# Moving output stores from ScalarE's DMA ring into GpSimd's, with the instruction order planned anew

## The chip, the cores and the metric

One core of one Trainium2 chip. The metric is the device time of one execution in microseconds; a kernel is quoted by the median of its runs. A ratio below is the mean time of one kernel's fast runs over the mean of the other kernel's fast runs of the same rounds, so it is not quite the ratio of the medians. "Slow" runs (here, runs over 1.5% above the fastest of the same kernel) are left out of ratios. Each ratio comes with a 95% interval. By a margin of 2% every experiment below but two counts as "same" as the kernel before (5 is slower, 6 is unclear); smaller differences are claimed only where the interval leaves out 1. The profile's span is some 2 us shorter than the device time of the same run.

## The reference, cut to what matters

```python
# 4 sequences, 8 heads, 768 positions, head size 64
scores = q @ k.T / 8 - slope[h] * dist             # a local window of 96 positions and 8 global ones
a = softmax(where(keep, scores, -1e9))
x = (a @ v).transpose(0, 2, 1, 3).reshape(3072, 512)
h = x @ w_in                                       # 512 -> 2048
out = (h - tanh(h)) @ w_out                        # 2048 -> 512, float32, [3072, 512]
```

The kernel cuts the 3072 rows into 24 tiles of 128. A tile's attention touches only its own and the preceding block of keys (and the 8 global ones), so the two dense layers are most of the matmul work. Two words recur: a "ring" is the queue of the transfers (DMA) that one engine issues, and an "eviction" copies a finished product out of PSUM, the memory in banks that matmuls write to.

## The kernel before

Every engine's instruction order is decided while the kernel is built: `plan()` plays through all operations with assumed durations and always takes next the one that could start first. Only these parts matter here (cuts are marked):

```python
opool = ctx.enter_context(tc.tile_pool(name="opool", bufs=4))     # four output tiles
kpool, bpool = ...                                                # qk: 7, kq: 5 buffers
...
def load_bf(u, nm):                                # q, k, v of tile u: GpSimd's ring, cast to bf16
    ... nc.gpsimd.dma_start(out=dst..., in_=by_head)
def a_DT(u):                                       # transpose of q and k by DMA: SyncE's ring
    nc.sync.dma_start_transpose(out=qk[u]..., in_=kq.pop(u)...)
def m2_e(u, part, eng):                            # eviction: PSUM -> ot, on ScalarE or VectorE
    ots[u] = opool.tile([P, DM], FP32, name="ot")
    copy_on(eng)(out=ots[u][:, lo:hi], in_=os_.pop((u, part)))
def store(u, part):                                # ot -> HBM, 256 KB
    eng = nc.sync if u == NU - 1 else nc.scalar
    eng.dma_start(out=out[...], in_=ots[u][:, lo:hi])
...
bufs = {"mo": 3, "kq": KQ, "p0": 3, "p1": 3, "x": 3, "xT": NG, "g": NG, "th": 3, "ot": 4}
```

With four `ot` buffers, the eviction of tile u has to wait until the store of tile u-4 has landed. The plan knows this rule.

The softmax here doesn't subtract the row's maximum and nothing guards it: scores larger than these inputs give would overflow.

Of the kernel before, what the change touches and what calls it, by code (L numbers as in the profile page):

```python
# [15 lines left out]
def kernel(  # L16
# [11 lines left out]
    nc = tc.nc  # L28

    B, H, S, Dh = q.shape  # L30
# [3 lines left out]
    NU = B * NQ  # L34
# [147 lines left out]
    ops = {}  # L182
    w_in_r = moe_w_in.rearrange("(c p) f -> p c f", p=P)
    w_out_r = moe_w_out.rearrange("(c p) d -> p c d", p=P)
    PE, ACT, DVE, POOL, SP = ENG.PE, ENG.Activation, ENG.DVE, ENG.Pool, ENG.SP
# [6 lines left out]
    def op(key, eng, us, fn, after=(), take=(), give=(), hold=(), free=(), pri=0, dma=0.0, alt=None, at=None, slack=0.0):  # L192
        ops[key] = dict(
            key=key, at=at, slack=slack, eng=eng, us=us, fn=fn, alt=alt, after=[a for a in after if a is not None],
            take=list(take), give=list(give), hold=list(hold), free=list(free), pri=pri, dma=dma,
        )
# [258 lines left out]

    def store(u, part):
        lo, hi = parts(u)[part]
        eng = nc.sync if u == NU - 1 else nc.scalar
        eng.dma_start(out=out[SEQ[u] * P : (SEQ[u] + 1) * P, lo:hi], in_=ots[u][:, lo:hi])


    AHEAD = 5.5
    YIELD = 0.0
    HALVES = 99
    EB = 2
    INF = 1.0e9
    NUDGE = {
        ('AV', 21): -0.3,
        ('E', 12, 1): 0.3,
        ('E', 13, 0): 0.3,  # L470
        ('E', 13, 1): -0.6,
        ('E', 14, 1): -0.6,
        ('E', 17, 0): -0.15,
        ('E', 17, 1): -0.15,
        ('E', 18, 1): 0.15,
        ('E', 21, 1): 1.0,
        ('E', 9, 1): -0.3,
        ('M', 14, 1): 0.3,
        ('M', 20, 0): 1.0,
        ('M', 9, 1): 1.0,  # L480
        ('R', 15): 0.6,
        ('R', 9): -0.3,
        ('S', 3, 0): 0.15,
        ('S', 6, 0): 1.0,
        ('S', 7, 0): 0.6,
        ('V', 16): -0.15,
        ('V', 19): -0.6,
        ('V', 4): -0.3,
        ('X', 6): 0.15,
        ('Xe', 9): -0.3,  # L490
        ('ev', 7, 0): 1.0,
        ('g', 1, 6): 0.3,
        ('g', 11, 6): 0.6,
        ('g', 13, 14): 0.3,
        ('g', 2, 2): 0.6,
        ('g', 7, 14): 1.0,
        ('g', 7, 8): 0.6,
        ('g', 9, 2): 1.0,
        ('m1', 12, 0): 0.6,
        ('m1', 4, 4): -0.3,  # L500
        ('m1', 4, 8): -0.15,
        ('m1', 5, 0): -0.3,
        ('m1', 5, 4): -0.3,
        ('m1', 5, 8): -0.15,
        ('m1', 6, 2): 0.6,
        ('m1', 8, 6): 1.0,
        ('m1', 9, 8): 0.6,
        ('m2', 1, 2): 1.0,
        ('m2', 10, 0): 1.0,
        ('m2', 11, 0): -0.3,  # L510
        ('m2', 12, 3): 0.3,
        ('m2', 15, 1): 0.3,
        ('m2', 2, 1): 1.0,
        ('m2', 21, 1): 0.6,
        ('m2', 3, 0): 0.6,
        ('m2', 3, 2): 1.0,
        ('m2', 5, 3): 1.0,
        ('m2', 7, 1): 0.3,
        ('m2', 7, 3): 0.3,
        ('m2', 8, 0): 1.0,  # L520
        ('st', 12, 0): 0.6,
        ('st', 8, 0): 1.0,
        ('th', 6, 10): -0.6,
        ('th', 7, 10): 0.3,
        ('th', 9, 8): 0.15,
    }
    SLACK_DT, SLACK_DX = 4.0, 4.0
    WARM = (1.1, 7.0)
    COLD = 6.3
    FETCH = (15.8, 0.9)  # L530
    T_ROWS, T_LD, T_W, T_ST, T_DT, T_DX = 0.67, 0.89, 1.3, 0.7, 1.75, 0.9
    LOADS = "ttttiiitiiiotoooioitooo"
    first, n_of = [], {"t": 0, "i": 0, "o": 0}
    for c in LOADS + "t" * NU:
        if n_of[c] < (NU if c == "t" else WJ):
# [12 lines left out]
    for it in first:  # L548
# [3 lines left out]
        u = it[1]  # L552
        for nm in ("vf", "kf", "qf") if u == 0 else ("kf", "qf", "vf"):
            key = ("ld", nm, u)
# [4 lines left out]
            after = []  # L559
            if nm == "vf" and u >= B + NV:  # L560
# [3 lines left out]
                 after=after, take=["kq"] if nm == "kf" else [], slack=0.15)  # L564
# [36 lines left out]
    for u in range(NU):  # L601
# [8 lines left out]
        if u < PE_T:  # L610
            t_us = 0.47 if PLAIN <= u < ROWS else 0.24
            apart = u < APART
            for j, r in ((1, rk), (0, rq)):
# [5 lines left out]
                     lambda eng, u=u, j=j: a_Te(u, j, eng),  # L619
# [40 lines left out]
        b, at, n_b = block_of(u)  # L660
# [9 lines left out]
    for g, us in enumerate(groups):  # L670
        b, o, n, _ = shape1(g)
# [10 lines left out]
    for u in range(NU):  # L682
        g = group_of[u]
        last_f = {f: f0 for f0, m in chunks(g) for f in range(f0, f0 + m)}
        n_u = 4 * len(parts(u))
        for n in range(n_u):
            part, qq = divmod(n, 4)
            lo, hi = parts(u)[part]
            op(("m2", u, n), PE, 4 * ((hi - lo) / 2400.0 + 0.0025), lambda u=u, n=n: m2(u, n),
               after=[("out", (4 * qq + 3) // FJ)] + [("g", g, f) for f in sorted({last_f[f] for f in range(4 * qq, 4 * qq + 4)})],  # L690
               take=["mo"] if u < EARLY2 and qq == 0 else [], hold=[(("m2", u, part), 1)] if qq == 0 else [],
               give=["g"] if n == n_u - 1 and ends_block(u) else [], pri=2)
        for part in range(len(parts(u))):
            alt = [(DVE, 0.3)] if part else [(ACT, 0.5), (DVE, 0.56)]
            flex(("ev", u, part), alt, lambda eng, u=u, part=part: m2_e(u, part, eng),
                 after=[("m2", u, 4 * part + 3)], take=["ot"] if part == 0 else [],
                 give=["mo"] if u < EARLY2 else [], free=[("m2", u, part)], pri=1)
            op(("st", u, part), SP if u == NU - 1 else ACT, 0.1 if u == NU - 1 else 0.4, lambda u=u, part=part: store(u, part), after=[("ev", u, part)],
               give=["ot"] if part == len(parts(u)) - 1 else [], dma=T_ST)


    def plan():
# [18 lines left out]
                b[i : i + n] = [INF] * n  # L721
            return at, got

        ring = {SP: [0.0, []], POOL: [5.8, []]}
        share = {SP: 0.5, POOL: 0.5}
        done, start, width = {}, {}, {}
        f1 = f2 = 0.0
        queues = {}
        for u in range(NU):
# [14 lines left out]
        while ready or any(queues.values()):  # L744
# [11 lines left out]
                    cand.append((qu[0], 10 ** 6 + name[1]))  # L756
            due = INF
            for key in ready:
                if key not in since:
                    since[key] = max([0.0] + [start[a[1]] if a[0] == "issue" else done[a] for a in ops[key]["after"]])  # L760
                if key[0] == "S" and len(ops[key]["hold"]) > 2:
                    due = min(due, since[key] + YIELD)
            for key, n in cand:
                o = ops[key]
                eng = o["eng"]
                if o["alt"]:
                    eng = min(o["alt"], key=lambda x: free[x[0]] + 0.6 * x[1])[0]
                t = free[eng]
                via = POOL if o["eng"] is POOL else SP
                if o["dma"] and len(ring[via][1]) >= 8:  # L770
                    t = max(t, sorted(ring[via][1])[-8])
                if key not in since:
                    since[key] = max([0.0] + [start[a[1]] if a[0] == "issue" else done[a] for a in o["after"]])
                t = max(t, since[key])
                if key[0] == "m1" and t >= due:
                    continue
                if best is not None and round(t + NUDGE.get(key, 0.0), 3) > best[0][0]:
                    continue
                if o["hold"]:
                    w = find(o["hold"])[0]  # L780
                    if w is None:
                        continue
                    t = max(t, w)
                for p in set(o["take"]):
                    n_p = o["take"].count(p)
                    if len(avail[p]) < n_p:
                        t = None
                        break
                    t = max(t, sorted(avail[p])[n_p - 1])
                if t is None:  # L790
                    continue
                c = (round(t + NUDGE.get(key, 0.0), 3), o["pri"], n)
                if best is None or c < best[0]:
                    best = (c, key, t, eng)
# [10 lines left out]
            if o["at"]:  # L805
                done[key] = o["at"]
            elif o["dma"]:
                via = POOL if o["eng"] is POOL else SP
                mine, other, part = ring[via], ring[SP if via is POOL else POOL], share[via]
                begin = max(mine[0], end + (1.0 if via is SP else 1.97))  # L810
                both = min(max(0.0, other[0] - begin), o["dma"] / part)
                mine[0] = begin + o["dma"] + both * (1 - part)
                if begin < FETCH[0] <= mine[0]:
                    mine[0] += FETCH[1]
                other[0] += both * part
                done[key] = mine[0] + (0.8 if via is SP else 0.45) + o["slack"]
                mine[1].append(done[key])
            else:
                done[key] = end + LAT[o["eng"]]
            if o["hold"]:  # L820
# [11 lines left out]
                    continue  # L832
                bank[banks[label] : banks[label] + width[label]] = [done[key]] * width[label]
            for p in o["take"]:
                avail[p].remove(min(avail[p]))
            for p in o["give"]:
                avail[p].append(done[key])
            order.append((t, key))
            if key[0] == "m1":
                queues["m1", min(key[1], EARLY)].pop(0)  # L840
# [74 lines left out]
```

## Time and profile before

215.21 us (median of 4 runs, 214.77 to 215.94).

| view | before | how to read it |
|---|---|---|
| span | 212.3 us | first to last instruction |
| TensorE busy | 203.8 us | near the limit; the gaps are what a change of order can win |
| TensorE waiting for DMA transposes | 1.9 us in 2 waits | the only stalls in mid-kernel |
| share of the 16 DMA engines in 46 to 73 us | 1.92 packets in flight on average | full; loads, transposes and stores compete |
| landing of a store, median and longest | 3.4 and 8.6 us | no eviction waits for one. The median is over all 26 store transfers; the 12 issued before 132 us, while the rings are full, took 6.1 to 8.6 us |

Lines of this profile stand in the prediction.

### The profile page before, as it was taken

The page shows a single profiled execution, that of the slowest core. Times are in us where ns is not written, and L with a number is a line of the kernel's source. Part 1 is how long each engine was busy: PE and PEld are TensorE (multiplying, and loading weights), DVE is VectorE, ACT ScalarE, POOL GpSimd, SP SyncE. Part 2 cuts the span into 40 slices and gives each one's busy share as a digit, 9 for nine tenths or more (in the row PEclk, how much of TensorE's full clock was granted, in tenths as well). Part 3 has the DMA queues.
Part 4 walks back from the last instruction along what each step waited for, and adds up shares of the span by engine and source line. Part 5 has one row for each costly group of instructions (what it writes and reads, how often), then busy time and mean ns, then how long its engine had stood idle before and what let it go on. Part 6 is the DMA issues. An engine that isn't in the chain of part 4 may idle for free.

```text
span 212.3 us, 5296 instructions
## 1 busy us (share of the span) xinstructions
PE 203.8 (96%) x2172; PEld 145.4 (68%) x2198; DVE 132.1 (62%) x269; ACT 120.4 (57%) x184; POOL 71.9 (34%) x92
## 2 busy tenths in 40 slices
PE   7899999999799899999999999999999999999994
PEld 2679995984466767577677578757755786666754
DVE  6579796656475777385667487757655594343611
ACT  4777865553446786487358465667545773444410
POOL 8995676667344365345342700000000000000000
PEclk9999999999999999999999999999999999999999
DMA  5999999999999999999999999212362220110112
GB/s 181 182 189 177 180 203 180 187 157 167 159 158 186 151 137 181 144 181 184 153 169 164 165 142 193 50 74 53 99 112 90 77 49 0 52 51 16 37 49 100
DMA packets 106073, 27.49 MB, mean 129 GB/s; under 512 B 94656, under 2 KB 103104, under 8 KB 106048
## 3 DMA queue, kind: packets, MB, share of 16 engines
q0 software_dynamic: 74048, 13.11, 84.9%
q1 hardware_dynamic: 28144, 7.48, 26.6%
q10 hardware_dynamic: 3856, 6.56, 9.7%
q8 instruction: 17, 0.28, 0.6%
q14 instruction: 8, 0.07, 0.1%
HBM read 27.26 MB, written 6.29 MB: 158 GB/s over the span
## 4 chain that ended last, share of the span: by engine, by line
PE 82%; DMA 13%; DVE 1%; issue 1%; POOL 0%; ACT 0%; SPq 0%; DVEq 0%
PE ps L410 38%; PE ps L444 32%; DMA qk<-kq 6%; DMA kq<-in_q_dram 5%; PE ps L314 5%; PE ps L342 2%; DMA kf<-in_k_dram 2%; PE ps L346 2%; PE ps L277 1%; PE ps L281 1%; PE ps L369 1%; PE ps L165 1%; POOL kq L242 0%; DVE kh L296 0%; DVE g L429 0%
## 5 line engine op out<-in xcount | busy, mean ns | idle before, releaser
L410 PE MATMUL ps<-xT,w_in_bf 128*128 128x256 bf16 (+1 forms) x960 | 93.0, 251 | 0.1
L444 PE MATMUL ps<-w_out_bf,g 128*128 128x512 bf16 (+3 forms) x391 | 87.3, 362 | 1.6 <-issue 0.5
L410 PEld LDWEIGHTS <-w_in_bf 128*128 128x128 bf16 x960 | 77.5, 98 | 13.3 <-DMA w_in_bf<-in_moe_w_in_dram 0.3
L429 DVE TENSOR_TENSOR g<-ps,th 128x512 bf16<-128x512 f32 (+1 forms) x102 | 64.9, 656 | 28.5 <-ACT th L422 27.8
L422 ACT ACTIVATE th<-ps 128x512 f32<-128x512 f32 (+1 forms) x102 | 56.8, 573 | 38.1 <-PE ps L410 35.0
L444 PEld LDWEIGHTS <-g 128*128 128x128 bf16 x416 | 37.9, 98 | 33.7
L323 ACT ACTIVATE pd<-ps 128x1024 bf16<-128x1024 f32 x24 | 24.4, 1024 | 14.0 <-PE ps L314 14.0
L236 POOL DMA_DIRECT2D vb<-in_v_dram x24 | 21.4, 894 | 14.3 <-DMA kq<-in_k_dram 4.6
L242 POOL DMA_DIRECT2D kq<-in_k_dram x20 | 17.7, 886 | 23.6 <-DMA qk<-kq 16.4
L323 ACT ACTIVATE po<-ps 128x1024 bf16<-128x1024 f32 x20 | 20.2, 1023 | 6.1 <-PE ps L314 6.1
L242 POOL DMA_DIRECT2D kq<-in_q_dram x20 | 17.7, 886 | 7.8 <-DMA vb<-in_v_dram 7.6
L329 DVE TENSOR_TENSOR pd<-pd,mk 128x1024 bf16<-128x1024 bf16 x20 | 13.8, 690 | 6.2 <-ACT pd L323 6.2
L355 DVE TENSOR_TENSOR x<-ps,rden 128x512 bf16<-128x512 f32 x24 | 16.6, 692 | 0.8
L454 ACT COPY ot<-ps 128x512 f32<-128x512 f32 x16 | 9.4, 585 | 13.7 <-PE ps L444 13.7
L329 DVE TENSOR_TENSOR po<-po,mk 128x1024 bf16<-128x1024 bf16 x20 | 13.7, 687 | 2.7 <-ACT po L323 2.7
L342 PE MATMUL ps<-vb,pd 128*128 128x65 bf16 x192 | 14.1, 193 | 0.0
L342 PEld LDWEIGHTS <-pd 128*128 128x128 bf16 x192 | 12.5, 98 | 1.4 <-issue 0.2
L454 DVE COPY ot<-ps 128x512 f32<-128x512 f32 (+3 forms) x10 | 5.8, 585 | 12.0 <-PE ps L444 11.9
L314 PEld LDWEIGHTS <-qk 64*128 64x128 bf16 x288 | 8.1, 94 | 7.0 <-issue 4.0
L314 PE MATMUL ps<-qk 64*128 64x128 bf16 x288 | 10.8, 217 | 1.9 <-DMA qk<-kq 1.9
L346 PE MATMUL ps<-vb,po 128*128 128x65 bf16 x160 | 12.4, 193 | 0.0
L346 PEld LDWEIGHTS <-po 128*128 128x128 bf16 x160 | 10.4, 97 | 1.1
(48 smaller groups left out, 81.9 us busy)
## 6 DMA issues: line engine op xcount, KB each, us to landing
out_dram<-ot ACTq DMA_DIRECT2D x23, 256.0 KB, 6.1
vb<-in_v_dram POOLq DMA_DIRECT2D x24, 128.0 KB, 10.9
kq<-in_k_dram POOLq DMA_DIRECT2D x22, 128.0 KB, 11.2
kq<-in_q_dram POOLq DMA_DIRECT2D x22, 128.0 KB, 11.2
w_in_bf<-in_moe_w_in_dram POOLq DMA_DIRECT2D x8, 256.0 KB, 8.3
w_out_bf<-in_moe_w_out_dram POOLq DMA_DIRECT2D x8, 256.0 KB, 8.7
kf<-in_k_dram SPq DMA_DIRECT2D x2, 256.0 KB, 4.5
qf<-in_q_dram ACTq DMA_DIRECT2D x2, 256.0 KB, 3.7
```

The source lines that it names most:

```text
L236: i = nc.gpsimd.dma_start(out=v_of(u)[:, :, 0:Dh], in_=by_head)
L242: i = nc.gpsimd.dma_start(out=dst.rearrange("p (h d) -> p h d", d=Dh), in_=by_head)
L314: nc.tensor.matmul(s[:, slot(2 * p + hh), :], kT(prev_of[u] if o else u)[r, p, :], qk[u][r, 0, p, :], start=u >= B, stop=True, skip_group_ ...
L323: nc.scalar.activation(pr[u, o].rearrange("q (a h) f -> q a h f", a=2)[:, part], sc[u, o][:, part, :].rearrange("q a (h f) -> q a h f", f= ...
L329: nc.vector.tensor_tensor(out=pr[u, o], in0=pr[u, o], in1=mk[:, :, mask_of(u, o) - 1, :], op=ALU.mult)
L342: nc.tensor.matmul(dst, pr[u, 0][:, slot(h), :], v_of(u)[:, h, :], start=True, stop=last,)
L346: nc.tensor.matmul(dst, pr[u, 1][:, slot(h), :], v_of(prev_of[u])[:, h, :], start=False, stop=True,)
L355: nc.vector.tensor_tensor(out=xs[u].rearrange("q (a h) d -> q a h d", a=2), in0=t[:, :, :, 0:Dh], in1=rden.to_broadcast([P, 2, H // 2, Dh] ...
L410: nc.tensor.matmul(t[:, (f - f0) * n : (f - f0 + 1) * n], w_in_bf[j][:, c, fo : fo + P], xT[b][:, c, o : o + n], start=(c == 0), stop=(c = ...
L422: nc.scalar.activation(h_view(ths[g, f0], g, m), h_view(hs[g, f0], g, m), AF.Tanh, bias=0.0, scale=1.0)
L429: nc.vector.tensor_tensor(out=gs[b][:, f0 : f0 + m, o : o + n], in0=h_view(hs.pop((g, f0)), g, m), in1=h_view(ths.pop((g, f0)), g, m), op= ...
L444: nc.tensor.matmul(os_[u, part][:, 0 : hi - lo], gs[b][:, f, t * P : (t + 1) * P], w_out_bf[f // FJ][:, f % FJ, lo:hi], start=(f == 0), st ...
```

## The change

The intent is to take the stores out of the competition that delays the transposes: 21 of 24 go into GpSimd's ring, behind the loads, and the planner now follows all three rings as fluids that share the DMA engines, re-estimating every landing at each issue. The 58 hand-found nudges make room for two, and the loads of weights are ordered a little differently.

```diff
-        eng = nc.sync if u == NU - 1 else nc.scalar
+        eng = nc.sync if u == NU - 1 else nc.gpsimd if u < BY_POOL else nc.scalar    # BY_POOL = 21
...
     NUDGE = {
-        ('AV', 21): -0.3,
...                                                 # 57 more
+        ('AV', 8): -0.6,
+        ('T1', 0): 1.0,
     }
-    T_ROWS, T_LD, T_W, T_ST, T_DT, T_DX = 0.67, 0.89, 1.3, 0.7, 1.75, 0.9
-    LOADS = "ttttiiitiiiotoooioitooo"
+    T_ROWS, T_LD, T_W, T_ST, T_DT, T_DX = 0.67, 0.89, 1.3, 0.65, 1.05, 0.55
+    SHARE = {  # speed of (GpSimd, SyncE, ScalarE) rings, by which of them are active
...
+    LOADS = "tttitiiitiiootooiiotooo"
...
+        def fly(jobs, t, t_end): ...               # moves all transfers in flight forward
+        def fly_from(q, key, t, end): ...          # a new issue: new landings for all of them
```

More of the change, by code (lines that the diff above doesn't have):

```diff
@@ L457, in store @@
         lo, hi = parts(u)[part]
-        eng = nc.sync if u == NU - 1 else nc.scalar
+        eng = nc.sync if u == NU - 1 else nc.gpsimd if u < BY_POOL else nc.scalar
         eng.dma_start(out=out[SEQ[u] * P : (SEQ[u] + 1) * P, lo:hi], in_=ots[u][:, lo:hi])
     AHEAD = 5.5
+    BY_POOL = 21
     YIELD = 0.0
@@ L467 @@
     NUDGE = {
-        ('AV', 21): -0.3,
-        ('E', 12, 1): 0.3,
-        ('E', 13, 0): 0.3,
-        ('E', 13, 1): -0.6,
-        ('E', 14, 1): -0.6,
-        ('E', 17, 0): -0.15,
-        ('E', 17, 1): -0.15,
-        ('E', 18, 1): 0.15,
-        ('E', 21, 1): 1.0,
-        ('E', 9, 1): -0.3,
-        ('M', 14, 1): 0.3,
-        ('M', 20, 0): 1.0,
-        ('M', 9, 1): 1.0,
-        ('R', 15): 0.6,
-        ('R', 9): -0.3,
-        ('S', 3, 0): 0.15,
-        ('S', 6, 0): 1.0,
-        ('S', 7, 0): 0.6,
-        ('V', 16): -0.15,
-        ('V', 19): -0.6,
-        ('V', 4): -0.3,
-        ('X', 6): 0.15,
-        ('Xe', 9): -0.3,
-        ('ev', 7, 0): 1.0,
-        ('g', 1, 6): 0.3,
-        ('g', 11, 6): 0.6,
-        ('g', 13, 14): 0.3,
-        ('g', 2, 2): 0.6,
-        ('g', 7, 14): 1.0,
-        ('g', 7, 8): 0.6,
-        ('g', 9, 2): 1.0,
-        ('m1', 12, 0): 0.6,
-        ('m1', 4, 4): -0.3,
-        ('m1', 4, 8): -0.15,
-        ('m1', 5, 0): -0.3,
-        ('m1', 5, 4): -0.3,
-        ('m1', 5, 8): -0.15,
-        ('m1', 6, 2): 0.6,
-        ('m1', 8, 6): 1.0,
-        ('m1', 9, 8): 0.6,
-        ('m2', 1, 2): 1.0,
-        ('m2', 10, 0): 1.0,
-        ('m2', 11, 0): -0.3,
-        ('m2', 12, 3): 0.3,
-        ('m2', 15, 1): 0.3,
-        ('m2', 2, 1): 1.0,
-        ('m2', 21, 1): 0.6,
-        ('m2', 3, 0): 0.6,
-        ('m2', 3, 2): 1.0,
-        ('m2', 5, 3): 1.0,
-        ('m2', 7, 1): 0.3,
-        ('m2', 7, 3): 0.3,
-        ('m2', 8, 0): 1.0,
-        ('st', 12, 0): 0.6,
-        ('st', 8, 0): 1.0,
-        ('th', 6, 10): -0.6,
-        ('th', 7, 10): 0.3,
-        ('th', 9, 8): 0.15,
+        ('AV', 8): -0.6,
+        ('T1', 0): 1.0,
     }
-    SLACK_DT, SLACK_DX = 4.0, 4.0
+    SLACK_DT, SLACK_DX = 2.0, 2.0
     WARM = (1.1, 7.0)
@@ L530 @@
     FETCH = (15.8, 0.9)
-    T_ROWS, T_LD, T_W, T_ST, T_DT, T_DX = 0.67, 0.89, 1.3, 0.7, 1.75, 0.9
-    LOADS = "ttttiiitiiiotoooioitooo"
+    T_ROWS, T_LD, T_W, T_ST, T_DT, T_DX = 0.67, 0.89, 1.3, 0.65, 1.05, 0.55
+    RING = 5.8
+    TAIL = {POOL: 0.45, SP: 0.8, ACT: 0.8}
+    SHARE = {
+        (True, False, False): (1.0, 0, 0), (False, True, False): (0, 1.0, 0), (False, False, True): (0, 0, 1.0),
+        (True, True, False): (0.36, 0.42, 0), (True, False, True): (0.5, 0, 0.42), (False, True, True): (0, 0.5, 0.42),
+        (True, True, True): (0.3, 0.29, 0.2),
+    }
+    LOADS = "tttitiiitiiootooiiotooo"
     first, n_of = [], {"t": 0, "i": 0, "o": 0}
@@ L697 @@
                  give=["mo"] if u < EARLY2 else [], free=[("m2", u, part)], pri=1)
-            op(("st", u, part), SP if u == NU - 1 else ACT, 0.1 if u == NU - 1 else 0.4, lambda u=u, part=part: store(u, part), after=[("ev", u, part)],
+            by = SP if u == NU - 1 else POOL if u < BY_POOL else ACT
+            op(("st", u, part), by, {SP: 0.1, POOL: 0.7, ACT: 0.4}[by], lambda u=u, part=part: store(u, part), after=[("ev", u, part)],
                give=["ot"] if part == len(parts(u)) - 1 else [], dma=T_ST)
@@ L722, in find, with fly @@
             return at, got
-        ring = {SP: [0.0, []], POOL: [5.8, []]}
-        share = {SP: 0.5, POOL: 0.5}
         done, start, width = {}, {}, {}
+        flying, landed, at_dma = {POOL: [], SP: [], ACT: []}, {POOL: [], SP: [], ACT: []}, [0.0]
+        def fly(jobs, t, t_end):
+            fin = {}
+            while t < t_end:
+                if FETCH[0] <= t < FETCH[0] + FETCH[1]:
+                    t = min(FETCH[0] + FETCH[1], t_end)
+                    continue
+                heads = [q for q in jobs if jobs[q] and jobs[q][0][1] <= t]
+                later = min([jobs[q][0][1] for q in jobs if jobs[q] and jobs[q][0][1] > t] + [t_end])
+                if not heads:
+                    t = later
+                    continue
+                rate = SHARE[tuple(q in heads for q in (POOL, SP, ACT))]
+                rate = {q: r for q, r in zip((POOL, SP, ACT), rate)}
+                dt = min([later - t] + [jobs[q][0][2] / rate[q] for q in heads])
+                if t < FETCH[0]:
+                    dt = min(dt, FETCH[0] - t)
+                t += dt
+                for q in heads:
+                    jobs[q][0][2] -= dt * rate[q]
+                    if jobs[q][0][2] < 1e-6:
+                        key = jobs[q].pop(0)[0]
+                        fin[key] = t + TAIL[q] + ops[key]["slack"]
+            return fin
@@ new lines, in fly_from @@
+        def fly_from(q, key, t, end):
+            busy = flying[POOL]
+            done.update(fly(flying, at_dma[0], t))
+            at_dma[0] = max(at_dma[0], t)
+            begin = end + (2.0 if q is POOL else 1.0)
+            if key[0] in ("T", "Xe"):
+                begin = t + (4.2 if busy else 2.2)
+            if q is POOL:
+                begin = max(begin, RING)
+            flying[q].append([key, begin, ops[key]["dma"], q])
+            landed[q].append(key)
+            done.update(fly({k: [list(j) for j in v] for k, v in flying.items()}, at_dma[0], INF))
@@ L727, in plan, with due_at, at_of @@
+        flies = {key: any(a[0] != "issue" and ops[a]["dma"] for a in o["after"]) for key, o in ops.items()}
+        def due_at(key):
+            if flies[key] or key not in since:
+                since[key] = max(
+                    [0.0] + [start[a[1]] if a[0] == "issue" else done[a] for a in ops[key]["after"]]
+                )
+            return since[key]
+        def at_of(x):
+            return done[x] if isinstance(x, tuple) else x
         f1 = f2 = 0.0
@@ L758, in plan @@
             for key in ready:
-                if key not in since:
-                    since[key] = max([0.0] + [start[a[1]] if a[0] == "issue" else done[a] for a in ops[key]["after"]])
                 if key[0] == "S" and len(ops[key]["hold"]) > 2:
-                    due = min(due, since[key] + YIELD)
+                    due = min(due, due_at(key) + YIELD)
             for key, n in cand:
@@ L768, in plan @@
                 t = free[eng]
-                via = POOL if o["eng"] is POOL else SP
-                if o["dma"] and len(ring[via][1]) >= 8:
-                    t = max(t, sorted(ring[via][1])[-8])
-                if key not in since:
-                    since[key] = max([0.0] + [start[a[1]] if a[0] == "issue" else done[a] for a in o["after"]])
-                t = max(t, since[key])
+                if o["dma"] and len(landed[eng]) >= 8:
+                    t = max(t, done[landed[eng][-8]])
+                t = max(t, due_at(key))
                 if key[0] == "m1" and t >= due:
@@ L788, in plan @@
                         break
-                    t = max(t, sorted(avail[p])[n_p - 1])
+                    t = max(t, sorted(at_of(x) for x in avail[p])[n_p - 1])
                 if t is None:
@@ L807, in plan @@
             elif o["dma"]:
-                via = POOL if o["eng"] is POOL else SP
-                mine, other, part = ring[via], ring[SP if via is POOL else POOL], share[via]
-                begin = max(mine[0], end + (1.0 if via is SP else 1.97))
-                both = min(max(0.0, other[0] - begin), o["dma"] / part)
-                mine[0] = begin + o["dma"] + both * (1 - part)
-                if begin < FETCH[0] <= mine[0]:
-                    mine[0] += FETCH[1]
-                other[0] += both * part
-                done[key] = mine[0] + (0.8 if via is SP else 0.45) + o["slack"]
-                mine[1].append(done[key])
+                fly_from(o["eng"], key, t, end)
             else:
@@ L834, in plan @@
             for p in o["take"]:
-                avail[p].remove(min(avail[p]))
+                avail[p].remove(min(avail[p], key=at_of))
             for p in o["give"]:
-                avail[p].append(done[key])
+                avail[p].append(key if o["dma"] and not o["at"] else done[key])
             order.append((t, key))
```

## The prediction

> **What bounds the kernel now.** I read the page first: busy shares and the slices.
>
> ```profile
> PE 203.8 (96%) x2172; PEld 145.4 (68%) x2198; DVE 132.1 (62%) x269; ACT 120.4 (57%) x184; POOL 71.9 (34%) x92
> ...
> PE   7899999999799899999999999999999999999994
> ...
> DMA  5999999999999999999999999212362220110112
> ```
>
> TensorE is busy nearly everywhere; the dips are the start, the slices at 50 to 58 us and at 69 to 74 us, and the end. The DMA row is full until about 132 us and nearly empty afterwards. So there are two limits: matmul work throughout, and transfers early on. Next I priced the matmul work from start-to-start spacing, since a busy mark hides how densely PE is fed. In the chain of waits, in its undisturbed late part:
>
> ```profile
> 186.00 0.87 PE ps L410 x8
> 186.87 0.86 PE ps L444 x4
> ```
>
> That is 109 ns for a first-layer matmul of 256 columns and 215 ns for a second-layer one of 512. From the same chain: 56 ns for 128 columns, 0.78 us for 24 score matmuls (32.5 ns each), 0.46 us for 16 probability-times-V matmuls (29 ns). The sum: 576 x 0.109 = 62.8; 384 x 0.056 = 21.5; second layer (24 tiles x 16 x 512 columns) 82.9; scores 352 x 0.0325 = 11.4; PV 352 x 0.029 = 10.2; transposes and bias matmuls about 8. Together **196.8 us** (the page has fewer second-layer matmuls than the program, 391 of 416; some records are missing). I call "offset" the clock minus the work already done. The last matmul ends at 209.5 us, so the offset ends at 12.7 us; a tail of 2.8 us (last eviction and store) makes the span of 212.3.
>
> Where does the offset grow? Summing the work in front of each score run in the program's order and comparing with the trace: 8.3 at 21 us, 8.5 at the scores of tile 6 (48.9 us), 9.9 at those of tile 7 (55.6), 11.2 at those of tile 10 (71.8), 12.7 at the end. The last 138 us cost only 1.5 us. PE's own waits name the two jumps, and the chain names the path into the second:
>
> ```profile
> PE ps L314 <- DMA qk<-kq: 1.9, 2, 1.2
> ```
>
> ```profile
> 46.37 0.86 POOL kq L242
> 47.23 11.45 DMA kq<-in_q_dram
> 58.79 0.04 issue
> 58.83 12.90 DMA qk<-kq
> 71.73 0.05 issue
> 71.78 0.62 PE ps L314 x16
> ```
>
> Tile 10's q needed 11.45 us to land and its DMA transpose 12.90 us more; for 24 us no matmul stood on this path. The DMA view of 46 to 73 us shows who shared the engines (columns: packets, MB, share):
>
> ```profile
> q0 software_dynamic: 14191, 1.79, 128.1%
> q1 hardware_dynamic: 5217, 1.30, 43.6%
> q10 hardware_dynamic: 720, 1.31, 19.3%
> ...
> out_dram<-ot ACTq DMA_DIRECT2D x4, 256.0 KB, 7.8
> ```
>
> q0 is GpSimd's ring (loads), q1 SyncE's (transposes), q10 ACT's: 1.31 MB there is five stores. Over 5 to 41 us q0 alone moved 6.48 MB (0.18 MB/us); here it got 1.79 MB in 27 us (0.066 MB/us).
>
> **What the Trainium skill says.** "DMA: Bandwidth & Descriptors", section "Queues, rings and completion order": each DMA engine round-robins between the queue rows it has work for, by packet. The view above agrees: three rows were served at once and q0 fell to about a third. Same page, section "Issuing engines are not separate DMA queues": rings of different engines end on the same 16 DMA engines. Hence the change cannot remove a byte; it only decides whom a store delays. "Perfetto Trace Analysis", section "Identifying the Most-Contended Engine": matmul occupancy is a bad measure of headroom. The trace agrees: PE is 96% busy, yet the spacing sum says 12.7 us of offset. "SBUF — State Buffer", the note on the "DVE blocks DMA" trap: descriptors of GpSimd's ring can be held up by VectorE copies. Here a GpSimd issue takes 0.70 to 0.93 us throughout, so no such stall shows; a store issued there should cost about that.
>
> **The change, part by part.** (1) 21 of 24 stores leave ACT's ring for GpSimd's. ACT loses 21 issues of 0.34 us = 7.1 us, GpSimd gains 21 of about 0.8 = 17 us. ACT is 57% and GpSimd 34% busy: nothing on the path.
>
> (2) A store in GpSimd's ring queues behind loads. From the built order: stores 0 and 1 stand after the loads of tile 11, stores 2 to 5 after those of tile 16, 6 to 10 between later loads, the last ten after all loads. So between 46 and 72 us only two stores compete instead of five, and those two behind the loads that tile 10 and 11 need. Cost of a store now: by packet time 19.3 / 191 of 27 us over five = 0.55 us; by bytes 1.31 / 4.44 of 27 us over five = 1.6 us. I choose 1.3 (an estimate; q0 took 6 us per tile there, and this size closes its account). Stores 0 and 1 preceded tile 10's q: it lands 2.6 us earlier, near 56.2. Its transpose, with no store beside it, should take nearer 8 to 9 us than 12.9: landing at 65 to 67.
>
> (3) The reordered plan. PE work in total is the same (4398 rows in both orders). Work ahead of the scores of tile 7 goes from 45.7 to 47.6 us, of tile 10 from 60.6 to 58.0, of tile 12 from 76.4 to 77.3. With offset 8.6, tile 7's scores are due at 56.2, after their transpose (55.6 before, about 1 us earlier now): the first stall, 1.4 us of offset, should go. Tile 10's are due at 66.6 against 65 to 67: most of the second stall, 1.3 us, goes. **Gain up to 2.5 us.**
>
> (4) The start: bias matmuls are hoisted ahead of the first transposes, and weights come earlier. But between 5 and 41 us the ring is full in both kernels with the same bytes, and from 24 us on PE needs w_in 4, 5 and w_out 0, 1 just as they land (24.5 and 27 us, from the trace's packets). So the start gives 0.2 us at most.
>
> (5) The four ot buffers. The eviction of tile u needs the store of tile u-4 landed. Formerly stores landed in 3.4 us (median); behind loads they take 10 to 13. Store 2 follows tile 16's V load (issued at 80.6 us before; I estimate 76 to 78 now) and lands at 85 to 89. Eviction 6 is wanted when 73.2 us of work are done, 82 us; VectorE reaches it near 84. VectorE takes its work in order, so it would stand up to 4 us; PE can go on to the scores of tile 12 (work 77.3, clock 86.2), which need six PSUM banks. PE's loss: 0 to 3.5 us, I take 1.1. The planner put this eviction after PE work 76 in its merged order, so it has seen the delay and filled around it, which speaks for the low half.
>
> Sum: 2.5 + 0.2 - 1.1 = 1.6 us less; 215.2 - 1.6 = 213.6. I say **213.7 us**.
>
> **Rivals.** A: no new wait. The offset stays near 8.8 through 90 us; 2.5 to 3 us are gained: 212.3 to 212.8. For it: the planner now models all three queues; the loads of tiles 17 and later are over 10 us ahead of need. Against: the ring's latency of 13 us where stores 2 to 5 stand. B: the wait moves from the transposes to the ot buffers, and VectorE blocks for 4 us; 215 to 217. For it: GpSimd's ring is FIFO and four stores stand in a row; stores (2 KB rows) share the ring with 256-byte pieces of loads that run at 0.066 MB/us beside transposes. Against: the order leaves VectorE work in front. C: 58 old nudges had been tuned to real stalls; without them small waits of 0.2 to 0.4 us return in many runs: 1 to 3 us, 214 to 217. Against: before's last 138 us had hardly any stall to tune away, and the work per tile there far exceeds its DMA. D: transfers are hidden anyway: the removed waits are only 2.3 us, so nothing beyond 1.5%.
>
> **Range and chances.** Faster by over 2% means under 211.0, a gain of 4.2 us; everything identified is 2.7. That needs gain in the start or in the late spacing: 0.06. Slower by over 2% means 219.5, several stalls at once: 0.04. Within 2%: 0.90. Range: 211.5 (all stalls gone and a better start) to 216.3 (rival B in full).
>
> **What would show it.** Right if: PE's waits on the DMA transposes fall from 1.9 us to under 0.7; the busy time of PE in 46 to 73 us rises from 24.75 to over 26; q10 carries nothing but the start's loads until the last tiles; the last matmul ends at about 208 us. Step 5: VectorE's idle time before its evictions (L454), with a DMA store as what ended it, between 82 and 90 us; over 3 us with a PE hole near 87 is rival B. Step 4 is wrong if the scores of tile 6 start clearly before 47.9 us (their work is 39.4). The prediction fails if the transposes remain slow without the stores (then stores were not the cause of the 12.9 us), or if the late part's drift of 1.5 us changes by more than 1 us.

## The result, and the profile after

223.43 us (median of 4 runs, 221.81 to 225.18; one of them slow), against 215.21. Ratio 1.0353, interval 1.0288 to 1.0419: **slower by 3.5%**.

The head of the page of the changed kernel (busy time by engine, then three rows of slices of 5.5 us):

```profile
PE 205.1 (93%) x2167; PEld 145.6 (66%) x2198; DVE 129.7 (59%) x265; ACT 121.9 (55%) x188; POOL 83.8 (38%) x113
...
PE   7799999999997999059999999999999999999994
...
PEclk9999999999999999859999999999999999999999
DMA  5999999999999999999999999407241212110112
```

One slice of TensorE reads 0, the next 5, and the granted clock dips in the same place. Everything else is nearly as full as before. The waits of 84 to 97 us (total, count, longest) name it:

```profile
DVE ot L454 <- DMA out_dram<-ot: 9.5, 1, 9.5
...
PE ps L314 <- DVE ot L454: 7.5, 1, 7.5
```

VectorE stood 9.5 us, once, at an eviction whose output buffer was still being stored, and TensorE stood 7.5 us behind it (7.7 us if the last matmul before it is priced by its usual spacing). The chain of waits in 76 to 100 us (start, duration, what):

```profile
78.73 17.01 DMA out_dram<-ot
...
95.76 0.70 DVE ot L454
96.46 0.04 issue
96.51 0.61 PE ps L314 x8
97.12 1.85 PE ps L410 x8
```

This is store 2: issued at 78.7 us, landed 17.0 us later. Eviction 6 needs its buffer. VectorE works in order, so a piece of the first layer of tiles 8 and 9 (h - tanh(h)) and the score masks behind that eviction waited too, and their PSUM banks stayed taken. TensorE's own lines of 88 to 101 us show where it had to stop, in the middle of the score run of tile 12, which needs six banks and got four:

```profile
88.34 0.62 PE L314 MATMUL ps<-qk 64*128 64x128 bf16 x16
96.51 0.61 PE L314 MATMUL ps<-qk 64*128 64x128 bf16 x8 [7.54 <-DVE ot L454]
97.10 1.87 PE L410 MATMUL ps<-xT,w_in_bf 128*128 128x256 bf16 x8
```

Eight first-layer matmuls take 1.87 us here; at 85.65 us, at full clock, eight took 1.04 us in such a view. The view by stretches (start, end, length, busy time of five engines, granted clock, DMA share, GB/s) says why:

```profile
96.50:99.70 3.20, 2.98 (x18) 1.95 (x19) 1.22 (x3) 1.62 (x2) 2.82 (x4) 0.50 1.94 120
```

The granted clock fell to half at 92.9 us, inside the hole, and stayed there until 99.7 us. The Trainium skill, "TensorE: Matmul & The Clock Gate", Part 1, says that TensorE goes to half clock after an idle window of about 3.4 us. This trace agrees (the fall came 3.9 us after the last matmul's end), but shorter holes did it too: in mid-kernel the profiles show half clock exactly in the runs where TensorE once stood 2.3 us or longer (this one and experiments 5, 6, 9 and 10), and never where it stood 1.9 us at most.

The account, by the prediction's "offset" (clock at a tile's first score matmul minus the matmul work ahead of it in the program, 196.8 us in all; one profiled run per column; rows 13 and 22 are the score runs that begin in that tile):

| first scores of tile | before | changed | new order, 8 buffers | new order, stores in ScalarE's ring | old order, stores in GpSimd's ring |
|---|---|---|---|---|---|
| 6 | 8.50 | 8.80 | 8.51 | 8.28 | 8.55 |
| 7 | 9.93 | 8.94 | 8.64 | 8.41 | 8.70 |
| 10 | 11.20 | 10.71 | 9.11 | 11.20 | 9.18 |
| 12 | 11.52 | 11.04 | 9.45 | 13.16 | 9.50 |
| 13 | 11.64 | **20.41** | 9.58 | 13.94 | 9.62 |
| 22 | 12.46 | 21.23 | 11.77 | 14.76 | 10.45 |

Up to tile 12 the changed kernel was 0.5 us ahead. Between tiles 12 and 13 it lost 9.37 us, where the kernel before loses 0.12: 7.7 us of hole, and 3.2 us at half clock, which costs 1.6 us. From tile 13 on it only carries the loss.

### The profile page after: what moved, and what is told of

The parts are those of the page before. It is cut to its first block, busy times and chain, and to the rows that moved or that the text cites. A ratio compares the mean times of both kernels' runs of the same rounds, so it can differ in the third digit from the quotient of the medians.

```text
span 221.5 us, 5335 instructions
## 1 busy us (share of the span) xinstructions
PE 205.1 (93%) x2167; PEld 145.6 (66%) x2198; DVE 129.7 (59%) x265; ACT 121.9 (55%) x188; POOL 83.8 (38%) x113
## 4 chain that ended last, share of the span: by engine, by line
PE 66%; DMA 26%; POOL 4%; issue 2%; DVE 1%; POOLq 0%
PE ps L410 30%; PE ps L444 27%; DMA vb<-in_v_dram 11%; DMA out_dram<-ot 8%; DMA kq<-in_k_dram 7%; PE ps L314 4%; PE ps L342 2%; POOL vb L236 2%; POOL kq L242 2%; PE ps L346 1%; PE ps L281 1%; PE ps L369 1%; DVE ot L454 0%; PE ps L165 0%; PE ps L277 0%
## 5 line engine op out<-in xcount | busy, mean ns | idle before, releaser
L410 PE MATMUL ps<-xT,w_in_bf 128*128 128x256 bf16 (+1 forms) x960 | 98.0, 252 | 0.1
L444 PE MATMUL ps<-w_out_bf,g 128*128 128x512 bf16 (+3 forms) x386 | 91.8, 362 | 1.6 <-issue 0.2
L429 DVE TENSOR_TENSOR g<-ps,th 128x512 bf16<-128x512 f32 (+1 forms) x102 | 64.9, 655 | 39.5 <-ACT th L422 38.7
L459 POOL DMA_DIRECT2D out_dram<-ot x21 | 11.8, 562 | 92.8 <-ACT ot L454 77.5
L454 DVE COPY ot<-ps 128x512 f32<-128x512 f32 (+3 forms) x9 | 5.2, 572 | 18.6 <-DMA out_dram<-ot 9.5
L454 ACT COPY ot<-ps 128x512 f32<-128x512 f32 x17 | 9.9, 585 | 10.7 <-PE ps L444 10.7
```

Source lines behind the costliest of these rows:

```text
L410: nc.tensor.matmul(t[:, (f - f0) * n : (f - f0 + 1) * n], w_in_bf[j][:, c, fo : fo + P], xT[b][:, c, o : o + n], start=(c == 0), stop=(c = ...
L429: nc.vector.tensor_tensor(out=gs[b][:, f0 : f0 + m, o : o + n], in0=h_view(hs.pop((g, f0)), g, m), in1=h_view(ths.pop((g, f0)), g, m), op= ...
L444: nc.tensor.matmul(os_[u, part][:, 0 : hi - lo], gs[b][:, f, t * P : (t + 1) * P], w_out_bf[f // FJ][:, f % FJ, lo:hi], start=(f == 0), st ...
L454: copy_on(eng)(out=ots[u][:, lo:hi], in_=src)
```

## The experiments

Two theories at the start. **Ring theory:** the loss is that one wait for a buffer, made by a store that stands too far back in a ring. **Plan theory:** the new order, without its nudges, is itself worse. The last three columns of the table above belong to three of these runs. Each experiment's edit is against the changed kernel unless it says otherwise.

**1. Eight output buffers, order untouched.**

```diff
-    opool = ... tc.tile_pool(name="opool", bufs=4)
+    opool = ... tc.tile_pool(name="opool", bufs=8)
```

> The changed kernel, its order of instructions untouched, with eight output buffers in place of four, so that no eviction waits for the store of the tile four before it. Ring theory (the whole loss is the one wait of eviction 6 for store 2, 9.5 us on VectorE, 7.7 us hole on TensorE plus about 1.5 us of slow TensorE clock after it): no hole, no clock loss, time 213 to 215. Plan theory (the new order without the old nudges is itself worse): hole moves or spreads, time stays at 219 or more. If both share it, 216 to 218.

Measured: 216.1 us (214.12 to 216.61), ratio 1.0015. No eviction waits for a store any more, the clock stays at 1.0 in the profiled run, and the hole is gone. All that is left of TensorE's waits:

```profile
PE ps L410 <- DMA xT<-x: 1.3, 1, 1.3
PE ps L392 <- DVE zero L862: 1.0, 1, 1.0
PE ps L165 <- ACT mk L177: 0.9, 1, 0.9
```

The longest store still took 16.7 us to land; nobody needed it sooner. So the wait for the buffer carries the loss, not the landing as such. The median lies over the expected 213 to 215, where the text on record has a loss shared by both theories (216 to 218). The profiled run does not tell why, since it was the fastest (214.12): in it a transpose of x, not of q and k, made TensorE wait once, 1.3 us at 111 us, and the offset grew by 1.5 us. Of the three others, not traced, two have a mean clock of 0.992.

**2. Stores 2 to 5 from ScalarE's ring, at their place in the plan.**

```diff
-        eng = ... nc.gpsimd if u < BY_POOL else nc.scalar
+        eng = ... nc.gpsimd if u < BY_POOL and not 2 <= u <= 5 else nc.scalar
```

> The changed kernel, order of everything else untouched, but stores 2, 3, 4 and 5 are issued from ACT's ring at the same place of the plan. Ring theory: store 2 no longer stands behind the loads of tiles 14 to 16, lands some 4 to 9 us after its issue (about 80 us), eviction 6 does not wait, time 213 to 216. Plan theory: 219 or more.

Measured: 215.69 us (213.18 to 218.93), two of four runs slow; the two fast ones give 0.9917 (0.9868 to 0.9965). No wait for a buffer and no hole. Four stores out of 21 made the difference.

**3. The new order with all 21 stores back in ScalarE's ring: the plan alone.**

```diff
-        eng = ... nc.gpsimd if u < BY_POOL else nc.scalar
+        eng = ... nc.scalar
```

> The changed kernel's order with all of the 21 stores back in ACT's ring (the new plan alone). Ring theory: 213 to 216, near the kernel before, since the plan costs nothing by itself. Plan theory: 219 or more, all of the loss is in the order.

Measured: 217.16 us, ratio 1.0084 (1.0042 to 1.0125). Not the 219 of the plan theory, but above what the ring theory allowed. TensorE's waits show what it is:

```profile
PE ps L314 <- DMA qk<-kq: 4.2, 4, 1.6
```

The new order asks for the scores of tiles 8, 9, 11 and 13 when their transposes are only just due; with the stores in the third ring they come late, four times. This order needs the ring that it was planned for.

**4. The old order with the 21 stores in GpSimd's ring: the ring alone.** Against the kernel before:

```diff
-        eng = nc.sync if u == NU - 1 else nc.scalar
+        eng = nc.sync if u == NU - 1 else nc.gpsimd if u < 21 else nc.scalar
```

> The kernel before's order with the 21 stores issued from GpSimd's ring at the places its plan has them (the ring alone, without the new plan). Ring theory: stores 0 to 4 stand in the ring among the loads of tiles 10 to 14 and land 8 to 14 us after issue; evictions 4 to 8 may wait for a buffer and GpSimd for evictions; 217 to 225. Plan theory: the ring does nothing by itself, 214 to 216.

Measured: **212.58 us** (212.51 to 212.93), ratio 0.9872 (0.9845 to 0.9898). Both theories missed this: the ring theory had feared waits for buffers here too. TensorE waits for no q or k transpose at all; the DMA view of 46 to 73 us and the stretch itself:

```profile
q0 software_dynamic: 17725, 3.24, 160.1%
q1 hardware_dynamic: 5280, 1.31, 39.6%
```

```profile
46.00:73.00 27.00, 27.00 (x300) 17.49 (x298) 17.98 (x36) 16.13 (x23) 17.63 (x22) 1.00 2.01 171
```

TensorE is busy all of the 27 us (24.75 before). The transposes moved the same 1.31 MB, and q0 now also holds five stores (1.31 of its 3.24 MB): the loads moved 1.93 MB, against 1.79 MB before, at the same bytes of stores. Here the stores are issued singly, the first five at 47.7, 53.5, 60.4, 63.1 and 68.1 us, each 2 to 9 us after its eviction began; in the changed kernel store 2 was issued 31 us after its eviction. The longest landing was 12.9 us and no eviction was waiting for it.

Part of this gain may be clock. Eight of the 25 recorded runs of the kernel before that list a clock show a mean of 0.991 or 0.992, which is what one stretch of 3.41 us at half clock gives (estimate: 1.7 of 213 us; experiment 10's profile has such a stretch). None of the 16 runs of the old order with stores in GpSimd's ring (experiments 4, 11 and 12) is under 0.998.

**5. Store 2 alone at its late place; stores 3 to 5 from ScalarE's ring.** This tells two reasons for the 17 us apart: four stores in a row, or the place behind the loads.

```diff
-        eng = ... nc.gpsimd if u < BY_POOL else nc.scalar
+        eng = ... nc.gpsimd if u < BY_POOL and not 3 <= u <= 5 else nc.scalar
```

> The changed kernel, order untouched, stores 3, 4 and 5 issued from ACT's ring; store 2 stays in GpSimd's ring at its late place behind tile 16's loads. Row-of-four theory (store 2 took 17.0 us because three more stores followed it and slowed all): it lands after 10 to 12 us, VectorE waits 2 to 5 us, TensorE's hole is 0 to 3 us, time 215 to 218. Place theory (17 us come from the loads and transposes ahead of it): landing 15 to 17 us after issue, VectorE waits 8 to 10 us, the hole of 6 to 8 us stays, 221 to 224.

Measured: 222.43 us, ratio 1.0369. The chain of waits of this run:

```profile
79.41 15.34 DMA out_dram<-ot
...
94.77 0.70 DVE ot L454
...
95.52 0.61 PE ps L314 x8
```

Still 15.3 us, and the whole loss is there (VectorE stood 9.7 us, TensorE 7.8). The row of four falls as the main reason; the two flights differ by 1.7 us. (The test is not free of the other three stores: issued at 74.5, 78.1 and 78.5 us, they were in flight in ScalarE's ring at the same time.) What stood ahead is in the changed kernel's DMA view of the first part of store 2's flight, 78.7 to 88 us:

```profile
q0 software_dynamic: 5643, 0.71, 161.7%
q1 hardware_dynamic: 2055, 0.50, 60.3%
```

In these 9.3 us the ring moved 0.71 MB in 5643 packets, 126 bytes each: those are loads, at 0.076 MB/us, beside transposes. Only then do large packets come: 88 to 91.5 us moved 0.81 MB in 521 packets. The rest to the landing at 95.74 us was slow, 0.47 MB on all rings in 91.5 to 95.8 us. Two of the seven loads ahead, the last of tile 16, themselves landed only at 94.13 and 95.46 us, and between 72 and 105 us everything in this ring landed in the order of its issue; so the store ended right behind the loads, but why these last ones took so long no run shows.

**6. Five output buffers, order untouched: the dose.**

```diff
-    opool = ... tc.tile_pool(name="opool", bufs=4)
+    opool = ... tc.tile_pool(name="opool", bufs=5)
```

> The changed kernel, order untouched, five output buffers: eviction 6 reuses store 1's buffer, eviction 7 store 2's. One-wait theory: VectorE reaches eviction 7 some 6 us later in its order (about 91 us), so it waits for store 2 (landing near 94 to 95) about 3 to 4 us in place of 9.5; TensorE's hole 1 to 3 us; no drop of the granted clock or a small one; time 215.5 to 218. If the loss came from something else than the buffers, 221 to 224 as with four.

Measured: 219.14 us, ratio 1.0192 (1.0125 to 1.0260); VectorE stood 5.1 us at eviction 7, for the same store 2. The hole was half of the other, yet over half of the loss stayed, and more than I had expected. Stretches of the hole and of what followed:

```profile
91.00:94.70 3.70, 0.14 (x2) 0.00 (x0) 0.74 (x2) 0.60 (x1) 1.26 (x2) 0.88 1.71 163
94.70:100.60 5.90, 5.50 (x31) 3.08 (x31) 4.55 (x9) 0.60 (x1) 5.21 (x8) 0.50 2.47 138
```

The half clock lasted 6.83 us by the records in both kernels (92.90 to 99.73 in the changed one, 93.78 to 100.61 here), and 10.24 us in experiment 5. Each is a whole number of 3.41 us: two in these, three in experiment 5, one in experiments 9 and 10. Of the 6.83 us the long hole hid more than half; here 5.9 us came after the hole, 5.5 of them busy, which cost some 2.75 us. Holes of 3.6 and 0.4 us, plus 2.75, make all but 0.25 of the 7.0 us between tiles 12 and 13.

**7. Six buffers, in the planner too, which then plans anew.**

```diff
-    opool = ... bufs=4)
+    opool = ... bufs=6)
...
-    bufs = {..., "th": 3, "ot": 4}
+    bufs = {..., "th": 3, "ot": 6}
```

> Six output buffers in the pool and in the planner, so the plan is made anew for them. Buffers theory: no eviction waits for a store; time 212.5 to 216, like the run with eight buffers and the plan untouched. Plan theory: 217 or more.

Measured: 214.37 us, ratio 0.9973 (0.9902 to 1.0044). No wait for a buffer; one of 1.9 us for a transpose of x.

**8. Four buffers, but stores win where a load could be issued at the same time.**

```diff
-               give=["ot"] if part == len(parts(u)) - 1 else [], dma=T_ST)
+               give=["ot"] if part == len(parts(u)) - 1 else [], dma=T_ST, pri=-1)
```

> Four buffers as in the changed kernel, but where a store and a load could be issued at the same time the planner takes the store: store 2 comes after tile 11's loads begin, stores 3 to 5 between the loads of tiles 12 to 15, each one alone. Place theory: store 2 lands near 70 us, long before eviction 6; no wait for a buffer; 212 to 216. If moving stores ahead of loads delays the loads enough, TensorE waits for transposes by 1 to 3 us in the scores of tiles 10 to 12; 215 to 218.

Measured: 213.2 us (212.61 to 213.72), ratio 0.9938 (0.9873 to 1.0003), and TensorE waits for no DMA in the profiled run. Stores 0 to 4 now go at 45.9, 46.9, 49.2, 56.4 and 64.3 us. The cost I had allowed for, loads delayed by stores, did not show.

**9. Only stores 2 and 3 moved, from behind the loads of tile 16 to just before those of tile 12.**

```diff
     order, model_end = plan()
+    order.sort(key=lambda x: x[0])
+    late = [x for x in order if x[1] in (("st", 2, 0), ("st", 3, 0))]
+    order = [x for x in order if x not in late]
+    at = next(n for n, x in enumerate(order) if x[1] == ("ld", "kf", 12))
+    order[at:at] = [(order[at][0], key) for _, key in late]
```

> The changed kernel with four buffers and everything in its place except stores 2 and 3, which GpSimd issues just before the loads of tile 12 instead of just after those of tile 16. Place theory: store 2 lands before 72 us, eviction 6 does not wait, eviction 7 neither; no hole, no drop of the granted clock; 213 to 216. If something else in the order made the hole, VectorE still stands for several microseconds near 86 us and the time stays above 219.

Measured: 215.44 us, ratio 1.0015 (0.9945 to 1.0085). No eviction waits for a store. The profiled run was slow (a wait of 2.7 us for a transpose of x and 3.41 us at half clock are in it), so its other waits are not compared. Moving two of 21 stores takes the whole loss back, all else in its place. With experiment 4 this says what the cause is: not the ring, but the late place in it, behind the loads, together with four buffers.

**10 and 11. Controls: eight buffers in the old order,** first with the stores where they were, then with the stores in GpSimd's ring (experiments 1's and 4's edits).

> Control: the kernel before with eight output buffers, nothing else. No eviction of it waits for a store, so the buffers alone should give nothing: ratio to the kernel before 0.995 to 1.005, waits on the transposes 1.5 to 2.5 us as before.

Measured: 214.83 us, ratio 1.0008. More buffers give nothing to the kernel before. In the profiled run one transpose still cost TensorE 2.3 us, and half clock from 57.12 to 60.53 us followed, all of it on work: sixteen second-layer matmuls took 5.13 us, where the same sixteen take 3.62 in the kernel before.

```profile
56.53 0.62 PE L314 MATMUL ps<-qk 64*128 64x128 bf16 x16 [2.27 <-DMA qk<-kq]
...
57.49 5.13 PE L444 MATMUL ps<-w_out_bf,g 128*128 128x512 bf16 x16
```

> The kernel before's order, stores in GpSimd's ring, eight output buffers. If the four buffers cost nothing in that order, 212.5 to 213.0 and the same ratio as with four (0.987); if they had held something back, below 211.5.

Measured: 212.84 us, ratio 0.9912 (0.9868 to 0.9955). The four buffers cost nothing in that order.

**12. Experiment 4 again, five rounds, on the chip of 9 to 11.**

> Repeat, on the chip of this call and with five rounds, of the kernel before's order with stores in GpSimd's ring and four buffers: ratio 0.985 to 0.990 to the kernel before; faster than both kernels of the study.

Measured: 212.59 us (212.31 to 213.92), ratio 0.9913 (0.9869 to 0.9957). The median repeats to 0.01 us; the kernel before drew faster runs this time, so the ratio is just outside what I expected. This version beats both kernels, the kernel before by about 1%.

## Why the prediction was wrong

Predicted 213.7 us in 211.5 to 216.3, 0.04 for slower by over 2%; measured 223.43.

- **Step 5 failed: the flight of store 2.** The mechanism was right and named in full: eviction 6, store 2, VectorE in order, the scores of tile 12 and their six banks. The sizes were wrong. Store 2's issue was estimated at 76 to 78 us (78.7 measured); its flight at 10 to 13 us (17.0); its landing at 85 to 89 us (95.7); VectorE's wait at up to 4 us (9.5); TensorE's loss at 0 to 3.5 us with 1.1 taken (7.7 us of hole and 1.6 us of half clock, 9.3). The flight was put under what loads took before in the middle of the kernel (13 to 15 us in the DMA view of 46 to 73 us), for which the prediction gives no reason. At this place seven loads were ahead at 0.076 MB/us. And the 3.4 us that it gives for stores before is a median over the whole kernel; while the rings were full they took 6.1 to 8.6 us.
- **A term was missing:** a hole of a few microseconds halved the clock for 6.83 us (10.24 in experiment 5). The profile before does not show it, but the Trainium skill, "TensorE: Matmul & The Clock Gate", Part 1, states a fall to half clock after idling; the sum should have had it beside any rival with a hole. It is the smaller part: rival B was 215 to 217 us on paper and 223 on the chip, and 1.6 us of that is clock; the rest is the length of the wait.
- **Trusting the planner's placement** ("it has seen the delay and filled around it") took the low half. Its landing times come from a model: built from the kernel, the plan has store 2 issued at 74.6 us, in flight for 10.8 and landed at 85.3, just in time for the eviction; on the chip it was issued 4 us later and flew 6 us longer. For stores 0 and 1 the same plan was right (landings at 64.1 and 64.9 us; 64.6 and 64.9 measured).
- **Steps 2 and 3 held in part.** A gain of up to 2.5 us in the tiles 7 to 12 was forecast. With the buffers out of the way the new order reaches tile 12 with an offset of 9.45 us, and the old order in the new ring with 9.50, against 11.52: 2.1 and 2.0 us. But in the changed kernel's own profiled run one wait of 1.2 us for a transpose remained at tile 10 (the prediction asked for under 0.7), TensorE was busy for 25.41 of the 27 us from 46 to 73 us (it asked for over 26), and only 0.5 us was in hand at tile 12. In experiments 1, 5 and 6, with the same order up to there, that wait was at most 0.3 us; so it comes and goes from run to run.
- **Step 4 held:** tile 6's scores start at an offset of 8.80 against 8.50, no gain at the start. **Step 1 held:** 21 issues more on GpSimd cost nothing that the waits show (mean 0.56 us each, not the 0.8 estimated).
- **Rival C** (lost nudges bring back small waits) is not needed: from tile 13 to 22 the changed kernel's offset grows by 0.82 us, and that of the kernel before by the same 0.82. That this order has nothing over the old one in the same ring is shown (1.0015 with eight buffers, against 0.9872 in the same rounds); why is only argued, by the waits for transposes of x that followed the late stores.

## What to carry to other kernels

Moving a transfer to another ring moves no byte less, but it changes who waits for whom. Before moving it, list for each transfer what waits for its landing, and take the landing time from the ring that it joins, with the queue ahead of it, not from the ring that it leaves. An in-order engine that waits for a buffer spreads that wait to everything behind it; here a little slack in buffers, or stores issued soon after their evictions, cost less than a landing time that had to be right.

## What the Trainium skill lacked or had wrong

- "DMA: Bandwidth & Descriptors", "Issuing engines are not separate DMA queues", says that issuing from several engines saves only the sequencer's time. Here the same stores from another ring, order untouched, gave ratios of 0.9872 and 0.9913, so the choice of ring can matter beyond that. That it does so by what a transfer takes turns with is argued, not shown.
- The same page, "Anatomy of one DMA", fits a GpSimd DMA as 2.0 us plus bytes over 436 GB/s, an estimate of 2.6 us for 256 KB. A nearly idle ring comes near it (median 2.3 us for the nine stores of 140 to 206 us in the changed kernel); behind the loads it was 17.0 us. The page has no term for the queue ahead.
- "TensorE: Matmul & The Clock Gate", Part 1, gives an idle window of about 3.4 us as what halves the clock. Here less was enough: half clock came with holes of 3.6 us (experiment 6, 2.6 us after the last matmul's end by the profile), 2.7 us (experiment 9, a slow run; 2.2 us after) and 2.3 us (experiment 10), though not with one of 1.9 us (experiment 7). These are single traces, and the ends of matmuls are modelled.
- No page says why the last loads ahead of store 2 landed as late as 94.1 and 95.5 us, while all rings moved 0.47 MB in 4.3 us; it stays open.
